# Two tiles for A's values, later output weights, a second tile turned by TensorE and a new order at the end

## The chip, the cores and the metric

The kernel runs on one core of one Trainium2 chip. The metric is the device time of one execution in microseconds, and where several runs are given, their median. TensorE (PE) multiplies, with its weight loads (PEld) running beside it; VectorE (DVE), ScalarE (ACT) and GpSimd (POOL) do the elementwise work; SyncE (SP) mostly issues transfers.

## The reference

Two attentions over the same 2048 positions, 640 wide, with 32 heads of 20, whose results are put side by side:

```python
# A: four segments of 512; causal inside a segment, plus a memory of the segments before
p = softmax(qs @ ks.T * 20**-0.5 + causal); a_dot = p @ vs
num = phi(qs) @ M;  den = phi(qs) @ z + 1e-6          # phi(t) = t + 1 if t > 0 else exp(t)
o = g * num / den + (1 - g) * a_dot                   # g = sigmoid(beta), per head
M += phi(ks).T @ vs;  z += phi(ks).sum()
A = concat(o) @ wo
# B: causal attention over a window of 256
B = softmax(where(0 <= i - j < 256, q @ k.T * 20**-0.5, -1e9)) @ v @ wo
out = concat([A, B], axis=-1)                         # 1 x 2048 x 1280, bf16
```

## The kernel before

The work is cut into eight chunks of 512 positions, A and B in turn: chunk 0 is A's first segment, chunk 7 is B's last. For each chunk PE makes q, k and v from the transposed x (`qk_job`, `v_job`), the scores of four heads at a time (`score_batch`, L814), ACT takes their exponentials from PSUM into tiles pt (L830), POOL (L869) and DVE (L847) mask them, PE multiplies them with v (`av` L883, `av_tile` L904), DVE transposes the result by 32x32 blocks (tt, L949), takes the reciprocal of the row sums (rr, L977), and POOL writes the normalised values to o (L987). A ones column beside each head's values in v yields the row sums. For A, `mem` adds the memory's part, and `dm_job` (L686) updates the memory from phi(k) and v.

A chunk's output product needs o with its features on the partitions. `final` does that through DRAM: four stores o to scr_o (L1021), one transposing transfer back (L1040, into a tile oT, which for chunk 7 is named xT), and then `final_job` multiplies with wo. In chunk 7 this is done for each of its four query tiles of 128 by itself. The last of them (qt = 3) takes another way, `last_job`: four matmuls with an identity `one` turn 128 features of o (L1121), sixteen small ones turn the other 32 (L1133), a DVE cast (L1125, into the free tile pq) and an ACT cast (L1139, into pkT) bring them to SBUF, and two halves of five matmuls each follow (`last_half`), cast by ACT (L1156) and DVE (L1159) and stored. The third tile (qt = 2) goes through DRAM and then also through `last_half`. The rows of the weights for `last_job` are in another order, so B's output weights are loaded twice: wo_B and wo_end, the latter into the place of wk_A.

A's values of a chunk lie in one tile vA, [128, 4, 696] in bf16: 16 heads in the first 348 columns, 16 in the second. `v_job` makes one half at a time: five matmuls into one of two PSUM banks, m0 and m1 (`bank`), and a DVE multiplication that empties the bank into vA (L733), four times. Then `v_squares` copies parts of that half to the tile vS by two transfers on SP (L757). A is read by `av` through `vof`, by `v_squares` and by `dm_job`. Semaphores are set by the framework from the tiles that each instruction reads and writes: instructions on the same tile wait for one another, where one of them writes.

What PE does next is written out in PLAN, a string: `k70*7` is seven steps of the job that makes the first piece of k in chunk 7, `v71` a step of the second half of its values, `o60` an output product of chunk 6 (`o72` of the third tile of chunk 7), `z0` a step of `last_job`; S or s is the next batch of scores, A the next product with v, M the next memory product. The small S and the large S differ in whether the matmuls up to the next score are done as four tiles of 32 columns (L930) or whole (L935). Jobs are generators that yield what they still wait for in the planner's model; other engines' instructions are put between PE's by the times of that model. Loads stand in a list, each with a gate (`self.known(n, what, piece)`, the modelled time of something, for wo_B the q piece 3 of chunk 2) and a due time; `next_load` issues them on SP in the order of the list.

What the change touches:

- PLAN, from the 254th us on (chunk 7's q, k and v and what comes after); before that it is as it was
- `v_job` L730, `v_squares` L750 to L757, `av` L883, `dm_job` L684 to L687, `vof` L1573 to L1576: the places that use vA and vS
- L1346 and L1347, L1357: making vA and vS, their ones columns (`v_ones`, L796 and L800) and zeros, on POOL
- L1372: wo_B's gate
- `final_job` L1054 to L1061, `last_job`, and `last` in `one_group` (L1602 to L1607): the third and the last tile

Of the kernel before, what the change touches and what calls it, by code (L numbers as in the profile page):

```python
# [10 lines left out]
BF16 = mybir.dt.bfloat16  # L11
F32 = mybir.dt.float32

P = 128
H = 32
DH = 20
# [67 lines left out]

def at_head(h):
    return VS * h + 12 * (h // 16)
# [181 lines left out]
class _K:  # L268
# [391 lines left out]
    def dm_job(self, seg, pkT, v):  # L660


        nc, f = self.nc, self.f
        yield self.known("pkT", seg)
        W = 4 * VS
        KT = self.KT
        spare = self.pkS
        nc.gpsimd.tensor_copy(
            out=spare[:].rearrange("p k (u r) -> p (k u) r", r=HD - DH),
            in_=pkT[:].rearrange("p k (u c) -> p (k u) c", c=HD)[:, :, DH:])  # L670
        there = f.on_pool(1000.0)
        own = [(lambda kt, m=m: pkT[:, kt, P * m:P * m + P], P, [m], m) for m in range(KT)]
        for some in (own, [(lambda kt, h=h: spare[:, kt, R2 * h:R2 * h + R2], R2,
                            [x for x in range(4) if MEM2[x][0] == h], None) for h in (1, 0)]):
            if some is not own:
                yield there
            yield "bank"
            dM, bi = self.bank()
            at = 0
            for lhs, rows, xs, g0 in some:  # L680

                gs = [g0] if g0 is not None else sorted(MEM2[x][1] for x in xs)
                n = W * len(gs)
                v0 = at_head(4 * gs[0])  # L684
                for kt in range(LT):
                    nc.tensor.matmul(dM[0:rows, at:at + n], lhsT=lhs(kt),  # L686
                                     rhs=v[:, kt, v0:v0 + n],  # L687
                                     start=(kt == 0), stop=(kt == LT - 1))
                f.on_pe("full", 4 * mm_ns(n), 4 * n, 0.0, 4)
                at += n  # L690
                if (rows, xs) != (some[-1][1], some[-1][2]):
                    yield 0.0

            rows = some[0][1]
            dv = dM[0:rows, 0:at].rearrange("p (x j c) -> p x j c", j=4, c=VS)
            if rows == P:
                mz = self.mz[:, 0:KT]
            else:
                mz = self.mz[0:rows, KT:].rearrange("p (b a) j c -> p a b (j c)", a=2)
                dv = dv.rearrange("p (a b) j c -> p a b (j c)", a=2)  # L700
            nc.vector.tensor_tensor(out=mz, in0=dv, in1=mz, op=ALU.add)
            self.close(bi, f.on_dve(100.0 + 1.04 * at, f.seen))
            f.open = False
        t = f.dve + 138.0
        yield self.known(2 * seg, "avs")
        blk, mz = self.blk, self.mz
        nc.gpsimd.tensor_tensor(out=blk[:, :, :, DH], in0=mz[:, :, :, DH], in1=self.bm[:],
                                op=ALU.mult)
        f.on_pool(150.0, t)
        nc.gpsimd.tensor_tensor(out=blk[:, :, :, 0:DH], in0=mz[:, :, :, 0:DH],  # L710
                                in1=self.ez[:].unsqueeze(3)
                                .to_broadcast([P, KT + 4, 4, DH]), op=ALU.mult)
        self.mark(f.on_pool(1700.0), "dm", seg)

    def v_job(self, n, half, w_ap, v, gate, needs):
        nc, f = self.nc, self.f
        for need in needs:
            yield need
        xT = self.xs[n]
        x0 = SH if gate else 0  # L720
        for tt in range(LT):
            yield "bank"
            ps, bi = self.bank()
            for kt in range(self.KT):
                self.wide(ps, xT[:, kt, x0 + tt * P:x0 + (tt + 1) * P],
                          w_ap[:, half, kt, :], 320, kt == 0, kt == self.KT - 1)
                if kt < self.KT - 1:
                    yield 0.0
            src = ps[:, 0:320].rearrange("p (h e) -> p h e", e=DH)
            dst = v[:, tt, HV * half:HV * half + 16 * VS].rearrange(  # L730
                "p (h e) -> p h e", e=VS)[:, :, 0:DH]
            if gate:
                nc.vector.tensor_tensor(  # L733
                    out=dst, in0=src,
                    in1=self.omg[:, 16 * half:16 * half + 16].unsqueeze(2)
                    .to_broadcast([P, 16, DH]), op=ALU.mult)
            else:
                nc.vector.tensor_copy(out=dst, in_=src)  # L738
            self.close(bi, f.on_dve(402.0, f.seen))
            f.open = False  # L740
        if not gate:
            self.v_ends(n, self.chunks[n][1], half, v)
        else:
            self.v_squares(n, half, v)
        self.used_x(n)

    def v_squares(self, n, half, v):


        f = self.f  # L750
        s = slice(HV * half, HV * half + HV)
        tok = v[0:SH, :, s].rearrange("p (a b) c -> p a b c", b=2)
        t = f.dve + 138.0

        def go():
            for odd in (0, 1):
                self.nc.sync.dma_start(  # L757
                    out=self.vS[SH * odd:SH * odd + SH, odd * 2:odd * 2 + 2, s],
                    in_=tok[:, :, odd, :])
                tl = f.on_dma(1, 410.0, t) + (1200.0 if n == 0 else 0.0)  # L760
            for g in range(4 * half, 4 * half + 4):
# [3 lines left out]
    def v_ends(self, n, c, half, v):  # L765
# [15 lines left out]
        def go():  # L781
# [3 lines left out]
            for g in range(4 * half, 4 * half + 4):  # L785
                self.mark(tl, n, "v", g)
        f.at(t, go)

    def v_tile(self, name, now=True):
        v = self.big.tile([P, LT, VW], BF16, name=name)  # L790
# [83 lines left out]
    def av(self, parts, g, vof):  # L874
# [4 lines left out]
        for n_, (ref, q0, nq, c0, pts) in enumerate(parts):  # L879
            v = vof(ref)  # L880
            for j in range(4):
                h = 4 * g + j
                nc.tensor.matmul(O[HD * j:HD * j + HD, q0:q0 + nq],  # L883
                                 lhsT=v[:, at_head(h):at_head(h) + HD],
                                 rhs=pts[j // 2][:, j % 2, c0:c0 + nq],
                                 start=(n_ == 0), stop=(n_ == len(parts) - 1),
                                 tile_position=(0, HD * j), skip_group_check=True)
# [160 lines left out]
    def final_job(self, n, wo, out2d, r0, col, t0, t1, there):  # L1048
# [2 lines left out]
        yield self.known("wo_A" if n % 2 == 0 else "wo_B", 0)  # L1051
        oT = self.oT[n]
        for tt in range(t0, t1):
            if n == len(self.chunks) - 1 and tt == LT - 2:  # L1054

                row = r0 + tt * P
                for hf in range(2):
                    yield "bank"
                    self.last_half(hf, lambda m: oT[:, m, tt * P:(tt + 1) * P], wo,
                                   out2d[row:row + P], col)  # L1060
                continue  # L1061
            while self.ring("ot", NOT) is None:
                self.stores[0]()
            yield self.ring("ot", NOT) - 700.0
# [40 lines left out]
        if t1 == LT:  # L1105
            self.mark(f.pe, "fin", n)

    def last_job(self, o, wo, out2d, r0, col, t):


        nc, f = self.nc, self.f
        yield t
        yield self.sc_free[-NSC]
        two = self.ps.tile([P, 2, 512], F32, name="sc", bufs=NSC)
        self.sc_free.append(f.pe + 3000.0)
        own = len(self.sc_free) - 1
        b0 = LT * (LT - 1)
        wide = two[:, 0, :].rearrange("p (j b t) -> p b j t", j=4, b=LT)
        one = self.one[:].rearrange("p (j t) -> p j t", j=4)
        for b in range(LT):  # L1120
            nc.tensor.matmul(wide[:, b], lhsT=o[:, b0 + b, 0:P], rhs=one, start=True, stop=True,  # L1121
                             skip_group_check=True)
            f.on_pe("full", mm_ns(P), P)
        oT = [self.pq[:, 0, 0:4 * P], self.pkT[:, 0, 0:P]]
        nc.vector.tensor_copy(out=oT[0], in_=two[:, 0, :])  # L1125
        self.sc_free[own] = td = f.on_dve(605.0, f.seen)
        yield self.sc_free[-NSC]
# [12 lines left out]
        self.sc_free[own] = ta = f.on_act(200.0, f.seen)  # L1140
        yield max(ta, td)
        oT = [oT[m // 4][:, P * (m % 4):][:, 0:P] for m in range(self.KT)]
        row = r0 + (LT - 1) * P
        for hf in range(2):
            yield "bank"
            self.last_half(hf, lambda m: oT[m], wo, out2d[row:row + P], col)
# [156 lines left out]
    def body(self, xA, A_wq, A_wk, A_wv, A_wo, A_beta, xB, B_wqkv, B_wo, out2d):  # L1303
# [39 lines left out]
        self.vL = big.tile([P, LT, VW], BF16, name="vL")  # L1343
        self.vU = big.tile([P, LT, VW], BF16, name="vU")
        self.vX = big.tile([P, VW], BF16, name="vX")
        self.vA = self.v_tile("vA")  # L1346
        self.vS = big.tile([P, LT, VW], BF16, name="vS")  # L1347
        self.consts_mz()
        nc.vector.memset(self.vL[:].bitcast(F32), 0.0)
        for t in (self.vU, self.vX):  # L1350
# [3 lines left out]
        nc.gpsimd.memset(self.kB[0][:, :, 0:SH], 0.0)  # L1354
        nc.gpsimd.memset(self.kB[0][:, KT:G, L:XC], 0.0)
        self.consts_ends()
        nc.gpsimd.memset(self.vS[:].bitcast(F32), 0.0)  # L1357
        f.on_pool(10500.0)
        f.on_dve(4500.0)
        k = len(self.loads)  # L1360
# [8 lines left out]
                                   None, 22000.0)  # L1369
        wo = {}  # L1370
        wo["A"] = self.load_w("wo_A", A_wo, self.known(0, "scored"), 6000.0)
        wo["B"] = self.load_w("wo_B", B_wo[0], self.known(2, "q", 3), 6000.0)  # L1372

        wo["end"] = self.load_w("wo_end", B_wo[1], self.known(NC - 1, "q", KT - 1), 9000.0,
                                self.wt["wk_A"][:].rearrange("p m k c -> p (m k c)").rearrange(
# [191 lines left out]
    def one_group(self, n, kind, c, g, what, parts, left, o_t, groups_done, scro, wo, out2d):  # L1567
# [3 lines left out]
        def vof(ref):  # L1571
            what, u = ref
            if what == "a":  # L1573
                return self.vA[:, u, :]
            if what in "st":
                return self.vS[:, 2 * (u % 2) + u // 2, :]  # L1576
            if what == "l":
                return self.vL[:, u % LT, :]
            if what == "u":
# [10 lines left out]
        if what == "tile":  # L1590
# [10 lines left out]

            def last(t):  # L1602
                if g0 == G - 4:
                    if qt == LT - 1:
                        self.fins.insert(0, self.job(self.last_job(o, wo["end"], out2d, c * L, col, t), "z0"))
                        return
                    self.final(n, o, scro[n], wo[kind], out2d, c * L, col, qt, qt + 1, t)  # L1607
            self.norm(tt, dst, False, last)
# [103 lines left out]
```

## Time and profile before

| what | us |
|---|---|
| median of three runs (332.38, 332.24, 330.19) | 332.24 |
| the profiled execution's own time | 332.54 |
| its span in the trace | 330.7 |
| busy: PE, PEld | 316.4, 176.2 |
| busy: ACT, POOL, DVE | 299.6, 265.4, 255.8 |
| granted PE clock | 1.00 of full |
| transfers: moved, packets | 47.45 MB, 76266 |

Times within the trace count from the start of the span; 1.84 us of the execution's time lie outside of it. In lists of waits a line names who waited, on what, and how long in total, how often and at most. In a timeline a line is a run of like instructions: start, duration, engine, source line, operation, tiles, count, and in brackets the idle time before it with what ended it. Engines with a q (SPq, ACTq) are queues that issue transfers. In the page the span is also cut into 40 slices of 8.27 us, with the busy share of each in tenths.

### The profile page before, as it was taken

Reading aid. Unit: us, or ns where it says so; the run is one execution under the profiler, and the core shown is the slowest. Engines: PE = TensorE matmul, PEld = TensorE weight load, DVE = VectorE, ACT = ScalarE, POOL = GpSimd, SP = SyncE. Lnnn points to the kernel's source line nnn. Section 1 sums busy time; section 2 is a strip of 40 time slices with the busy share of each in tenths; the row PEclk is TensorE's granted clock in tenths of the full one; section 3 lists DMA queues with packets and bytes.
Section 4 is the critical chain, followed back from the end, with each engine's and each line's share of the span. In section 5 each row is a group of like instructions: output and inputs, shape, how many; then the busy total and the mean of one; then the engine's idle time right before and its main releaser. Section 6 shows DMA issues by size and latency. Waiting matters only on the chain.

```text
span 330.7 us, 16968 instructions
## 1 busy us (share of the span) xinstructions
PE 316.4 (96%) x7195; PEld 176.2 (53%) x7195; DVE 255.8 (77%) x533; ACT 299.6 (91%) x333; POOL 265.4 (80%) x672
## 2 busy tenths in 40 slices
PE   7999999998999999999999999999999999999984
PEld 2454546555445455646653546456654445666652
DVE  6777767797977787999867897988777798876753
ACT  1979999998999998989999999899999999979962
POOL 8466679997759899976886999998975899989850
PEclk9999999999999999999999999999999999999999
DMA  7975945675589354165689146117868027397642
GB/s 210 388 250 135 194 138 108 150 193 159 135 214 217 67 115 132 22 141 147 138 216 174 33 86 157 50 32 154 147 181 186 14 54 185 107 233 159 109 127 80
DMA packets 76266, 47.45 MB, mean 143 GB/s; under 512 B 48382, under 2 KB 73182, under 8 KB 76190
## 3 DMA queue, kind: packets, MB, share of 16 engines
q1 hardware_dynamic: 75469, 45.71, 57.7%
q8 instruction: 56, 0.92, 1.2%
q10 hardware_dynamic: 720, 0.66, 0.7%
q14 instruction: 21, 0.16, 0.2%
HBM read 17.62 MB, written 16.96 MB: 105 GB/s over the span
## 4 chain that ended last, share of the span: by engine, by line
PE 36%; DVE 5%; ACT 3%; DMA 2%; POOL 2%; issue 1%; SPq 1%; ACTq 0%; DVEq 0%
PE m L935 19%; PE sc L814 7%; PE m L883 5%; ACT pt L830 3%; PE m L930 2%; DVE tt L949 2%; PE m L904 1%; DMA xT<-scr_o 1%; DVE pt L847 1%; DMA scr_o<-o 1%; POOL pt L869 1%; DVE kA L557 1%; POOL o L987 1%; DVE ot L1099 0%; PE m L686 0%
## 5 line engine op out<-in xcount | busy, mean ns | idle before, releaser
L830 ACT ACTIVATE pt<-sc 128x1024 bf16<-128x1024 f32 (+2 forms) x306 | 282.9, 1026 | 15.1 <-PE sc L814 12.9
L869 POOL TENSOR_SCALAR_AFFINE_SELECT pt<-pt 128x128 bf16<-128x128 bf16 (+1 forms) x512 | 178.0, 376 | 49.8 <-ACT pt L830 42.8
L949 DVE STREAM_TRANSPOSE tt<-m 128x512 f32<-128x512 f32 x88 | 61.2, 709 | 24.7 <-PE m L883 15.9
L987 POOL TENSOR_TENSOR o<-tt,rr 128x320 bf16<-128x320 f32 x64 | 48.5, 758 | 4.7 <-DVE rr L977 3.9
L814 PE MATMUL sc<-qB,kB 20*64 20x64 bf16 (+2 forms) x1728 | 39.9, 217 | 0.8 <-ACT pt L830 0.3
L935 PEld LDWEIGHTS <-xT 128*128 128x128 bf16 x296 | 26.7, 97 | 18.4 <-issue 6.1
L847 DVE TENSOR_TENSOR pt<-pt,ends 128x1024 bf16<-128x1024 bf16 (+2 forms) x50 | 36.4, 739 | 0.0
L1099 DVE CAST ot<-m 128x320 bf16<-128x320 f32 x58 | 28.1, 486 | 9.8 <-PE m L935 8.4
L814 PEld LDWEIGHTS <-kB 20*64 20x64 bf16 (+1 forms) x1728 | 22.2, 98 | 22.4 <-issue 20.5
L814 PE MATMUL sc<-qA,kA 20*64 20x64 bf16 (+4 forms) x1024 | 33.5, 237 | 0.5 <-ACT pt L830 0.4
L935 PEld LDWEIGHTS <-oT 128*128 128x128 bf16 x244 | 21.5, 97 | 12.5 <-issue 3.3
L814 PEld LDWEIGHTS <-kA 20*128 20x128 bf16 (+1 forms) x1024 | 13.4, 97 | 22.4 <-issue 21.3
L935 PE MATMUL m<-wBv,xT 128*128 128x320 bf16 x147 | 24.2, 299 | 0.9 <-DVE tt L949 0.4
L883 PE MATMUL m<-pt,vA 128*32 128x192 bf16 (+3 forms) x512 | 23.6, 274 | 0.2
L935 PE MATMUL m<-wo_A,oT 128*128 128x320 bf16 x125 | 21.0, 300 | 0.8 <-DVE kA L557 0.8
L935 PE MATMUL m<-xT,wBq 128*128 128x512 bf16 x82 | 21.4, 380 | 0.3 <-DVE tt L949 0.3
L935 PE MATMUL m<-xT,wBk 128*128 128x512 bf16 x81 | 20.7, 381 | 0.0
L935 PE MATMUL m<-wv_A,xT 128*128 128x320 bf16 x119 | 20.0, 300 | 0.2 <-DVE vA L733 0.2
L738 DVE CAST vB<-m 128x320 bf16<-128x320 f32 x32 | 15.6, 488 | 5.4 <-PE m L935 3.1
L935 PE MATMUL m<-wo_B,oT 128*128 128x320 bf16 x109 | 18.6, 300 | 0.8 <-DVE tt L949 0.4
L557 DVE CAST qB<-m 128x512 bf16<-128x512 f32 x20 | 13.8, 688 | 6.7 <-PE m L930 3.4
L935 PE MATMUL m<-xT,wk_A 128*128 128x512 bf16 x69 | 17.7, 379 | 1.2 <-DMA xT<-in_A_x_dram 1.1
(127 smaller groups left out, 460.2 us busy)
## 6 DMA issues: line engine op xcount, KB each, us to landing
out_dram<-ot SPq DMA_DIRECT2D x29, 160.0 KB
scr_o<-o SPq DMA_DIRECT2D x28, 160.0 KB
xT<-in_B_x_dram SPq DMA_DIRECT2D x8, 288.0 KB
xT<-in_A_x_dram SPq DMA_DIRECT2D x8, 256.0 KB
scr_pk<-e SPq DMA_DIRECT2D x15, 128.0 KB
vS<-vA SPq DMA_DIRECT2D x16, 87.0 KB
vL<-vB SPq DMA_DIRECT2D x8, 174.0 KB
scr_kA<-kA SPq DMA_DIRECT2D x16, 60.0 KB
```

The source lines that it names most:

```text
L557: nc.vector.tensor_copy(out=dst[:, m, at:at + L], in_=ps[:, :])
L738: nc.vector.tensor_copy(out=dst, in_=src)
L814: nc.tensor.matmul(ps[j // 2][h0:h1, j % 2, c0:c0 + nq], lhsT=k[rows, g, k0:k0 + h1 - h0], rhs=q[rows, g, q0:q0 + nq], start=True, stop=Tr ...
L830: nc.scalar.activation(out=pt[:, :, lo:hi], in_=ps[i][:, :, lo:hi], func=ACT.Exp, scale=self.scale)
L847: nc.vector.tensor_tensor(out=blk, in0=blk, in1=self.ends[:, c0, :].unsqueeze(1).unsqueeze(1) .to_broadcast([P, 2, n // SH, SH]), op=ALU.mult)
L869: nc.gpsimd.affine_select(out=blk, in_=blk, pattern=pat, compare_op=ALU.is_ge, fill=self.zero, base=base, channel_multiplier=mul)
L883: nc.tensor.matmul(O[HD * j:HD * j + HD, q0:q0 + nq], lhsT=v[:, at_head(h):at_head(h) + HD], rhs=pts[j // 2][:, j % 2, c0:c0 + nq], start= ...
L930: self.nc.tensor.matmul(ps[s, 0:n], lhsT=lhsT[:, s], rhs=rhs, start=start, stop=stop, tile_position=(0, HD * j), skip_group_check=True)
L935: self.nc.tensor.matmul(ps[:, 0:n], lhsT=lhsT, rhs=rhs, start=start, stop=stop, skip_group_check=True)
L949: self.nc.vector.transpose(out=tt[:], in_=O[:, :])
L987: nc.gpsimd.tensor_tensor(out=to[:] if add_to else to, in0=a, in1=b, op=ALU.mult)
L1099: nc.vector.tensor_copy(out=ot[:, 320 * hf:320 * hf + 320], in_=ps[:, 0:320])
```

## The change

It does four things. vA and vS become two tiles each, one for each half of 16 heads, and every use takes the half's tile with its offset. The gate of wo_B's load becomes q piece 0 of chunk 4. In chunk 7 the third tile (qt = 2) is also handed to `last_job`, with its own places in pq and pkT (second slices), the label z0 (the last tile is z1 now), and the weights wo_end; its four stores and the transposing transfer go. And the last fifth of PLAN is another order of the same kinds of steps. Before the 254th us PE's order is unchanged.

```diff
-    "A k70*2 S k70*5 v70*3 S v70*2 q70*4 s q70 A s M q70*6 s q70*4 A s k73*5 s v70*5 A s M "
...
-    "s o40*5 o50*3 s o50*2 o40*5 o50*2 s o50*3 A s o50*10 s A o50*2 s o50*9 s o50*9 s A o60*5 s "
-    "o60*5 o70*5 A o70 s o70*4 o60*5 s o60*5 o71*4 s o71*6 o60*2 s o60*6 A o60*8 A o60*4 o72*2 "
-    "z0*4 ")
+    "A k70*2 S k70*5 v70*3 S v70*2 q70*4 s q70 A M s q70*5 s A q70*5 s v70*5 k73*2 s k73*3 A s "
...
+    "A s o40*5 o50*5 s o40*5 o50*5 s A o50*4 s o50*6 s A o50*4 s o50*8 s o50*8 s A o60*5 s "
+    "o60*10 o70*5 s A o70*3 s o70*2 o60*7 s o60*8 o71*2 s o71*3 o60*2 A o60*3 z0 o71*5 o60 A "
+    "o60 z0 o60*3 z0 z1*2 z0 z1*2 ")
...
-                v0 = at_head(4 * gs[0])
+                v0 = at_head(4 * gs[0]) - HV * (gs[0] // 4)
...
-                                     rhs=v[:, kt, v0:v0 + n],
+                                     rhs=v[gs[0] // 4][:, kt, v0:v0 + n],
...
-            dst = v[:, tt, HV * half:HV * half + 16 * VS].rearrange(
+            own, c0 = (v[half], 0) if gate else (v, HV * half)
+            dst = own[:, tt, c0:c0 + 16 * VS].rearrange(
...
-        tok = v[0:SH, :, s].rearrange("p (a b) c -> p a b c", b=2)
+        tok = v[half][0:SH].rearrange("p (a b) c -> p a b c", b=2)
...
-                    out=self.vS[SH * odd:SH * odd + SH, odd * 2:odd * 2 + 2, s],
+                    out=self.vS[half][SH * odd:SH * odd + SH, odd * 2:odd * 2 + 2, :],
...
+    def half_tiles(self, name):
+        return [self.big.tile([P, LT, HV], BF16, name="%s%d" % (name, x)) for x in range(2)]
...
-            if n == len(self.chunks) - 1 and tt == LT - 2:
-                row = r0 + tt * P
-                for hf in range(2):
-                    yield "bank"
-                    self.last_half(hf, lambda m: oT[:, m, tt * P:(tt + 1) * P], wo,
-                                   out2d[row:row + P], col)
-                continue
...
-    def last_job(self, o, wo, out2d, r0, col, t):
+    def last_job(self, o, wo, out2d, r0, col, t, qt):
...
-        yield self.sc_free[-NSC]
+        yield lambda: self.sc_free[-NSC] if self.all_scored else None
...
-        b0 = LT * (LT - 1)
+        b0 = LT * qt
+        own_x = LT - 1 - qt
...
-        oT = [self.pq[:, 0, 0:4 * P], self.pkT[:, 0, 0:P]]
+        oT = [self.pq[:, own_x, 0:4 * P], self.pkT[:, own_x, 0:P]]
...
-        self.vA = self.v_tile("vA")
-        self.vS = big.tile([P, LT, VW], BF16, name="vS")
+        self.vA = self.half_tiles("vA")
+        for t in self.vA:
+            nc.gpsimd.memset(t[:, :, 0:16 * VS].rearrange("p t (h e) -> p t h e", e=VS)[
+                :, :, :, DH], 1.0)
+            nc.gpsimd.memset(t[:, :, HV - 12:HV], 1.0)
+        self.vS = self.half_tiles("vS")
...
-        wo["B"] = self.load_w("wo_B", B_wo[0], self.known(2, "q", 3), 6000.0)
+        wo["B"] = self.load_w("wo_B", B_wo[0], self.known(4, "q", 0), 6000.0)
...
-                    if qt == LT - 1:
-                        self.fins.insert(0, self.job(self.last_job(o, wo["end"], out2d, c * L, col, t), "z0"))
+                    if qt >= LT - 2:
+                        self.fins.insert(0, self.job(self.last_job(
+                            o, wo["end"], out2d, c * L, col, t, qt), "z%d" % (qt - LT + 2)))
```

More of the change, by code (lines that the diff above doesn't have):

```diff
@@ L750, in v_squares @@
         f = self.f
-        s = slice(HV * half, HV * half + HV)
-        tok = v[0:SH, :, s].rearrange("p (a b) c -> p a b c", b=2)
+        tok = v[half][0:SH].rearrange("p (a b) c -> p a b c", b=2)
         t = f.dve + 138.0
@@ L881, in av @@
             for j in range(4):
-                h = 4 * g + j
+                at = at_head(4 * g + j) - (HV * (g // 4) if ref[0] in "ast" else 0)
                 nc.tensor.matmul(O[HD * j:HD * j + HD, q0:q0 + nq],
-                                 lhsT=v[:, at_head(h):at_head(h) + HD],
+                                 lhsT=v[:, at:at + HD],
                                  rhs=pts[j // 2][:, j % 2, c0:c0 + nq],
@@ L1142, in last_job @@
         oT = [oT[m // 4][:, P * (m % 4):][:, 0:P] for m in range(self.KT)]
-        row = r0 + (LT - 1) * P
+        row = r0 + qt * P
         for hf in range(2):
@@ L1356, in body @@
         self.consts_ends()
-        nc.gpsimd.memset(self.vS[:].bitcast(F32), 0.0)
+        for t in self.vS:
+            nc.gpsimd.memset(t[:].bitcast(F32), 0.0)
         f.on_pool(10500.0)
@@ L1573, in vof @@
             if what == "a":
-                return self.vA[:, u, :]
+                return self.vA[g // 4][:, u, :]
             if what in "st":
-                return self.vS[:, 2 * (u % 2) + u // 2, :]
+                return self.vS[g // 4][:, 2 * (u % 2) + u // 2, :]
             if what == "l":
```

4 rows, old and new, of the table PLAN are left out of this document.

## The prediction

> **What bounds the kernel now.** I read the page first, then the waits over the whole span, then the waits and the timeline of 72 to 90 us and of 310 to 331 us, where the diff acts, and at last the busy time by windows.
>
> ```profile
> PE 316.4 (96%) x7195; PEld 176.2 (53%) x7195; DVE 255.8 (77%) x533; ACT 299.6 (91%) x333; POOL 265.4 (80%) x672
> PE   7999999998999999999999999999999999999984
> PEclk9999999999999999999999999999999999999999
> ```
>
> TensorE (PE) is busy for 316.4 of 330.7 us, nearly evenly, at the full granted clock. So time can come back only from the about 14 us in which PE stands, 4 of them before its first x and in the last writes, or from fewer matmuls, and the change removes no matmul. ScalarE (ACT), at 91%, is close behind: what PE gains in a stretch where ACT has no gap is lost again at the next score that needs a free bank. The waits name the stalls:
>
> ```profile
> DVE vA L733 <- DMA vS<-vA: 1.5, 1, 1.5
> PEld L883 <- DVE vA L733: 2.2, 3, 1.5
> ACT e L577 <- DVE kA L557: 0.9, 1, 0.9
> PE m L935 <- DVE kA L557: 0.8, 2, 0.5
> PE m L935 <- DMA xT<-scr_o: 0.8, 1, 0.8
> PE m L935 <- DVE pq L1125: 0.6, 1, 0.6
> ```
>
> The columns are total us, times and longest. The first line is one wait of VectorE (DVE) for a transfer; the next three are its consequences. The timeline places them (start, duration, in brackets the idle time before and its releaser):
>
> ```profile
> 73.17 2.07 SPq L319 DMA_DIRECT2D wo_B<-in_B_wo_dram  x2
> 75.33 1.33 SPq L757 DMA_DIRECT2D vS<-vA  x2
> 79.51 0.49 DVE L733 TENSOR_TENSOR vA<-m,omg 128x320 bf16<-128x320 f32 x1 [1.49 <-DMA vS<-vA]
> 80.06 0.29 PE L883 MATMUL m<-pt,vX 128*32 128x256 bf16 x4 [1.01 <-DVE vA L733]
> 81.91 0.57 PE L935 MATMUL m<-wo_A,oT 128*128 128x320 bf16 x3 [0.47 <-DVE kA L557]
> 81.95 1.06 ACT L577 ACTIVATE e<-kA 128x1024 bf16<-128x1024 bf16 x1 [0.93 <-DVE kA L557]
> 87.42 1.94 ACT L830 ACTIVATE pt<-sc 128x1024 bf16<-128x1024 f32 x2 [0.50 <-PE sc L814]
> ```
>
> SP, the transfer queue, issues B's 800 KB of output weights at 73.17 and only then the copy vS<-vA of half 0. That copy reads the tile vA, DVE's next instruction writes half 1 of the same tile, and so DVE stands until the copy has landed. PE then stands for a bank that DVE would have emptied (1.01), and again for kA (0.47), which DVE, without a gap from 79.51 to 87.72, reaches late. The other place is the end:
>
> ```profile
> 315.68 0.72 PE L935 MATMUL m<-wo_B,xT 128*128 128x320 bf16 x4 [0.84 <-DMA xT<-scr_o]
> 316.84 3.77 ACT L830 ACTIVATE pt<-sc 128x1024 bf16<-128x1024 f32 x4 [0.81 <-PE sc L814]
> 317.94 3.54 POOL L869 TENSOR_SCALAR_AFFINE_SELECT pt<-pt 128x256 bf16<-128x256 bf16 x8 [2.94 <-ACT pt L830]
> 321.40 0.12 PEld L904 LDWEIGHTS <-vB 128*32 128x32 bf16 x8 [0.26 <-DVE tt L949]
> 323.49 0.73 POOL L987 TENSOR_TENSOR o<-tt,rr 128x320 bf16<-128x320 f32 x1 [0.95 <-DVE rr L977]
> 324.26 0.23 PEld L1121 LDWEIGHTS <-o 128*128 128x128 bf16 x4 [0.32 <-POOL o L987]
> 324.72 0.68 DVE L1125 CAST pq<-sc 128x512 bf16<-128x512 f32 x1
> 325.46 0.72 PE L935 MATMUL m<-wk_A,pq 128*128 128x320 bf16 x4 [0.56 <-DVE pq L1125]
> ```
>
> PE waits for the transposed second tile (0.84), the last scores come late, so do the exponentials, POOL's masks, the last product with v, its normalisation, and the last tile's turning. Between the two places lies a stretch that ACT holds:
>
> ```profile
> 240.00:293.00 53.00, 52.13 (x1145) 28.15 (x1131) 41.91 (x91) 52.24 (x56) 45.49 (x120) 1.00 0.54 132
> ```
>
> Busy time here stands as PE, PEld, DVE, ACT, POOL: both PE and ACT are over 98% full.
>
> **Part 1, tiles for the halves.** DVE's write of half 1 no longer waits for the copy of half 0. The matmul that fills its bank is done by 77.5, so DVE goes on at 78.02, 1.49 earlier. The bank is empty at 78.51, before PE asks at 79.05: the 1.01 goes. kA, done at 81.86, comes at 80.37; PE asks at 81.44 - 1.01 = 80.43: the 0.47 goes too. That is 1.48. The bound above is DVE's own 1.49 and PE's two small stands after it (0.36 at 84.79 and 0.16 at 85.99), so 2.0; ACT can follow by its gaps, 0.93 + 0.50 = 1.43, before it is full. I take 1.4, the nearest limit. The bound below is 0, if the shift is met by a later wait of like size. The other fifteen copies cost nothing now: the list of waits has this one alone. In the prelude POOL does four memsets for vA instead of three and two for vS instead of one (0.67 + 0.51 and 1.25 in all before, same bytes); an additional one is 0.1 to 0.7, its work ends at 7.95 and its first mask starts at 10.28 after 2.34 of idleness: hidden, and 0 if that cover held only 0.7.
>
> **Part 2, wo_B later.** Two SP issues (2.07) and 800 KB leave 73.17 and go behind the last x load of the fifth chunk, 127.02 by the old times, where SP then has nothing until 138.68 and the transfer engines stand at a share of 0.30 over 120 to 140. At the old pace from issue to landing (the second half's issue ended at 75.23, the copy behind it had landed by 79.51) it is there by about 131 to 133; PE first reads it at 149.6. Cover 16 us or more: 0. At 73 the copy vS could now leave 2.1 earlier; with part 1 nobody waits for it at 79.51, so the gain is not counted twice. Either part alone should end the 1.49. SP's moves behind it (scr_qA at 76.75 and what follows) come up to 2.1 earlier: bounded by 0 and the 0.2 that PEld waits for scr_kA; taken as 0.
>
> The Trainium skill, "DMA: Bandwidth & Descriptors", Rules for kernel authors, advises to issue a transfer early and to wait on it late; by that the old place of wo_B, 76 us ahead of its use, is the better one, and part 2 could only lose. The trace disagrees here: the early place is what the copy stood behind.
>
> **Part 3, the third query tile by TensorE.** Added on PE: 4 matmuls of L1121 (0.40) and 16 of L1133 (0.30), as the last tile has now, 0.70. Added on DVE a cast of 0.68 like L1125's, on ACT one of 0.27 like L1139's. Removed on SP: four stores of scr_o (315.04 to 316.92) and a transpose issue (318.30 to 319.94). That transfer is hidden now: issued like the second tile's (issue 311.50, landed 315.63, 4.13) it lands near 322.43, and PE asks at 322.75. So nothing is saved by the removal itself. The 0.70 lies before the last tile's turning, where PE stands 0.32 for POOL's o, 0.18 and 0.26 earlier. The third tile's second half, 5 matmuls or 0.69, is kept for the 0.56 in which PE waits for DVE's cast. Cost between 0 and 0.70; the end is worked out with part 4.
>
> The Trainium skill, "Perfetto Trace Analysis", Transposes, wants such turns done as transposes, not as a standard matmul, which these 20 are. By it PE pays for arithmetic that it could skip, at most the 0.70, and the sum would be 0.7 smaller; the waits above say that most of the 0.70 falls into stands.
>
> **Part 4, the new order from 254 us on.** The numbers of matmuls and of changes between tile shapes stay as they are. To 311 us I give it 0: ACT runs from 240.23 to 292.84 without a break. The bound above is PE's short stands for ACT there, about 1.2; below, -0.7, one score asked late by as much as a batch (16 to 64 matmuls, up to 0.7). In the tail the second tile's ten matmuls move behind the last scores, so its transposed tile (315.63) is asked for at about 316.5: the 0.84 goes, and the 0.18 after it. The last scores start at 316.9 instead of 317.92, ACT's last four exponentials run without the 0.81, so ACT and POOL end about 1.15 earlier (POOL at 320.3 instead of 321.48). PE, from 317.3: 5 matmuls (0.137 each, 0.68), first product 0.86, 3 matmuls, turn 0.40, 6 matmuls, then the last product with v at 320.6 instead of 321.40. Its chain is unchanged (2.86 from that start to L1121): turning at 323.46, done 324.16, cast by 324.6; the third tile's second half ends at 324.85, and the last ten start there instead of 325.46. Gain 0.6. Bounds: 1.1 (the masks' whole shift) and 0 (the 0.7 of part 3 uncovered).
>
> **Sum.** 1.4 + 0 + 0.6 = 2.0. The profiled execution is 332.54 (span 330.7 and 1.84 around it), 0.30 over the median of 332.24 of the three runs, which lie from 330.19 to 332.38. 332.54 - 2.0 = 330.54; against the median 330.2 us.
>
> **Rivals.**
> A, absorbed: the 1.4 is given back before 254, at ACT or at a later wait of DVE, since PE arrives early at scores whose banks are taken. For it: ACT is 91% busy. Against: ACT has its own 1.43 in the same place, and a further gap of 1.26 at 210.39. Only the 0.6 is left, or less: 331.7.
> B, the order gives more: PE's stands for ACT to 311 (1.2) go too, ACT's gap of 1.95 at 294.79 shows that it would take the work. 332.24 - 3.3 = 328.9 and less.
> C, slower: the third tile's turning is put by DVE and PE ahead of the last tile's. Place: DVE's cast (0.68) between the last product and its transpose, and PE's 0.70 ahead of that product, with scores before 311 each asked late by up to 0.7. It decides if the first turning is ready only after about 320.6; each is then on the path in full, 1.4, with the 0.6 lost and the 0.84 kept since the second tile's data are late again: 332.24 - 1.4 + 1.4 + 0.8, about 333; 334.4 if part 1 is absorbed too, over 335.6 with two late scores on top. Against: that tile's o is written by 315.04, as its stores show, long before.
> D, part 1 does not do what it says: the wait at 79.51 remains through another dependency. With only the tail, 331.6; counted with A.
>
> **How the numbers follow.** Forecast (330 to 331.2) 0.5, A and D 0.22, B 0.16, C 0.12 (its worst 0.08). Within 1%, about what a measurement here can tell from no change, is 328.9 to 335.6. Forecast, A, D and most of C lie in it. Faster by over 1%: B's 0.16 and a little of the forecast, 0.2; slower by over 1%: the worst of C, 0.08; same 0.72. The range 328.3 to 332.7 leaves out the deep end of B and most of C.
>
> **What would show it.** Right if no DVE wait for vS<-vA remains, kA's wait at 81.4 is gone and PE reaches its 254th us 1.4 earlier; if wo_B is issued near 126 with no PE wait at its first use; if the 0.84 for xT is gone and the last ten matmuls follow the third tile's second half directly. Wrong if PE waits on ACT's pt before 254 grow by about 1 (A), if waits on ACT to 311 shrink by over 1 (B), or if DVE's second pq cast sits ahead of the last transpose (C).

## The result

The changed kernel takes 330.48 us in the median of 22 runs (329.76 to 331.63), against 332.42 us for the kernel before, also of 22 (329.65 to 336.27). The ratio is 0.9946, with a 95% interval of 0.9929 to 0.9963: 1.9 us less, a gain of half a per cent, clear of the noise and smaller than 1%. The forecast was 330.2. The profiled execution of the changed kernel took 330.69 with a span of 329.0, against 332.54 and 330.7. Medians are of all runs; ratios, and medians of several sets together, leave out the runs that lie more than 1.5% above the fastest of their kernel.

The total came out as forecast, its two terms did not. The early parts alone reach the whole gain, though I gave them 1.4, and of the 0.6 that I added for the end nothing shows on top of them.

### The profile page after: what moved, and what is told of

Same layout as the page of the kernel before. It is cut to its first block, busy times and chain, and to the rows that moved or that the text cites. A ratio compares the mean times of both kernels' runs of the same rounds, so it can differ in the third digit from the quotient of the medians.

```text
span 329.0 us, 16969 instructions
## 1 busy us (share of the span) xinstructions
PE 314.1 (95%) x7180; PEld 177.2 (54%) x7215; DVE 257.7 (78%) x534; ACT 299.8 (91%) x334; POOL 266.2 (81%) x674
## 3 DMA queue, kind: packets, MB, share of 16 engines
q1 hardware_dynamic: 74221, 45.38, 57.2%
## 4 chain that ended last, share of the span: by engine, by line
PE 48%; POOL 9%; ACT 7%; DVE 5%; issue 4%; POOLq 0%; ACTq 0%; DVEq 0%
PE m L939 25%; PE sc L818 10%; PE m L887 7%; ACT pt L834 6%; POOL pt L873 6%; PE m L934 5%; DVE tt L953 3%; POOL o L991 2%; PE m L908 1%; POOL u L991 1%; DVE pt L851 1%; PE m L686 0%; POOL rr L972 0%; ACT e L577 0%; POOL MZ L710 0%
## 5 line engine op out<-in xcount | busy, mean ns | idle before, releaser
L939 PEld LDWEIGHTS <-xT 128*128 128x128 bf16 x286 | 25.8, 97 | 17.7 <-issue 6.8
L939 PE MATMUL m<-xT,wBq 128*128 128x512 bf16 x73 | 20.6, 380 | 0.9 <-DVE tt L953 0.3
L939 PE MATMUL m<-xT,wBk 128*128 128x512 bf16 x70 | 19.6, 380 | 0.7 <-issue 0.3
L557 DVE CAST kB<-m 128x512 bf16<-128x512 f32 x20 | 13.6, 680 | 6.7 <-PE m L939 5.7
```

Of the source, the lines that this page charges most:

```text
L557: nc.vector.tensor_copy(out=dst[:, m, at:at + L], in_=ps[:, :])
L939: self.nc.tensor.matmul(ps[:, 0:n], lhsT=lhsT, rhs=rhs, start=start, stop=stop, skip_group_check=True)
```

## The profile after

The page first:

```profile
span 329.0 us, 16969 instructions
PE 314.1 (95%) x7180; PEld 177.2 (54%) x7215; DVE 257.7 (78%) x534; ACT 299.8 (91%) x334; POOL 266.2 (81%) x674
```

35 matmul records are missing from this trace (7180 against 7215 weight loads), so its PE time is some us too low; stages are measured on the weight loads below. The timeline around the old stall, with the same columns as before:

```profile
73.50 0.70 PE L939 MATMUL m<-wv_A,xT 128*128 128x320 bf16 x4 [0.48 <-DVE qA L557]
74.48 1.66 SPq L757 DMA_DIRECT2D vS<-vA  x2
77.97 0.48 DVE L734 TENSOR_TENSOR vA<-m,omg 128x320 bf16<-128x320 f32 x1
124.88 0.91 SPq L319 DMA_DIRECT2D wo_B<-in_B_wo_dram  x2
```

The copy vS<-vA leaves SP 0.85 earlier, nothing stands ahead of it, and DVE's next write of vA (third line) has no idle time in brackets any more; before, it stood 1.49 for the copy. The weights are issued at 124.88, and no wait for them appears anywhere. The first line is new, a wait of 0.48 for DVE's qA; it did not come again in other profiles of the same order. Busy time of 78 to 82 us (PE, PEld, DVE, ACT, POOL), the kernel before and then the changed one:

```profile
78.00:82.00 4.00, 2.52 (x122) 1.64 (x122) 2.48 (x7) 3.07 (x5) 2.68 (x7) 1.00 0.45 111
```

```profile
78.00:82.00 4.00, 3.91 (x130) 2.54 (x131) 3.97 (x12) 4.00 (x6) 3.50 (x8) 1.00 0.39 69
```

PE goes from 2.52 to 3.91 of 4.00, and DVE and ACT are full. The end of the changed kernel:

```profile
310.56 7.48 ACT L834 ACTIVATE pt<-sc 128x1024 bf16<-128x1024 f32 x8 [0.44 <-PE sc L818]
315.37 3.53 POOL L873 TENSOR_SCALAR_AFFINE_SELECT pt<-pt 128x256 bf16<-128x256 bf16 x8 [1.32 <-PE m L939]
318.34 0.69 DVE L1122 CAST pq<-sc 128x512 bf16<-128x512 f32 x1
319.04 0.12 PEld L908 LDWEIGHTS <-vB 128*32 128x32 bf16 x8 [0.26 <-DVE pq L1122]
321.90 0.40 PE L1118 MATMUL sc<-one,o 128*128 128x128 bf16 x4 [0.33 <-POOL o L991]
322.47 0.72 PE L939 MATMUL m<-wk_A,pq 128*128 128x320 bf16 x4
325.74 0.34 ACTq L1169 DMA_DIRECT2D out_dram<-ot  x1
```

ACT's two gaps (0.80 and 0.81) have become one of 0.44; the last eight exponentials run together, and POOL's last masks end at 318.90 instead of 321.48. The last product with v follows at 319.04 (321.40 before); of these 2.36 us, 1.36 are there already at the 5491st weight load (see below), ahead of the new order. The third tile's second half starts at 322.47, and PE no longer waits for the cast.

To see where time is won and lost in any of the kernels, I cut each trace at the same instructions. PE's order is equal in all of them up to 254 us, so the 16th, 1901st and 5491st weight load are the same work. The stages are a: 16th to 1901st load (the old stall lies in it); b: to the 5491st; c: to the start of the last product with v; d: to PE's last matmul; e: to the end of the issue of the last store; f: to the end of the span. All in us, each from one trace:

| kernel | 16th load at | a | b | c | d | e | f | c to f |
|---|---|---|---|---|---|---|---|---|
| before | 6.38 | 91.44 | 155.56 | 68.02 | 5.59 | 1.32 | 2.42 | 77.35 |
| changed | 5.86 | 90.11 | 156.05 | 67.03 | 5.69 | 1.34 | 2.89 | 76.95 |
| e1 halves alone | 6.22 | 89.55 | 155.41 | 67.42 | 5.59 | 1.31 | 2.43 | 76.75 |
| e2 gate alone | 5.87 | 89.55 | 156.02 | 67.32 | 5.59 | 1.32 | 2.42 | 76.65 |
| e3 halves and gate | 5.91 | 89.55 | 155.83 | 67.44 | 5.58 | 1.33 | 2.41 | 76.76 |
| e4 end alone | 5.92 | 91.13 | 156.11 | 67.06 | 5.70 | 1.33 | 2.89 | 76.98 |
| e5 new order, third tile by DMA | 5.89 | 89.67 | 155.90 | 66.80 | 8.20 | 1.25 | 2.43 | 78.68 |
| e6 old order, third tile turned | 6.08 | 89.56 | 156.49 | 66.82 | 6.77 | 1.40 | 2.86 | 77.85 |
| e7 new order from 309 us only | 6.33 | 89.61 | 155.80 | 67.01 | 5.70 | 1.33 | 2.89 | 76.93 |
| e8 changed again | 5.96 | 89.61 | 156.66 | 67.02 | 5.70 | 1.33 | 2.87 | 76.92 |
| e9 changed, more on SP | 5.86 | 89.55 | 155.90 | 67.08 | 5.70 | 1.33 | 2.43 | 76.54 |
| e10 second tile later | 5.81 | 90.01 | 155.74 | 67.12 | 5.59 | 1.32 | 2.42 | 76.45 |
| e11 halves and gate again | 6.25 | 89.84 | 156.68 | 67.28 | 5.59 | 1.32 | 2.42 | 76.61 |

Stage b is the same work in all rows and differs by 1.3 from trace to trace, and the first x comes in anywhere within 0.6: this is what a single time of these kernels can't see through. Where nothing in a stage was changed, the others repeat within about 0.1 to 0.6, but for the c of 68.02.

## Experiments on the early part

Each kernel was timed in 12 runs; the kernel before beside them had medians of 332.67 (e1 to e4), 332.20 (e5 to e8) and 332.22 (e9 to e11).

**e1, the halves alone.** Everything on vA and vS from the change, and nothing else of it:

```diff
-        self.vA = self.v_tile("vA")
-        self.vS = big.tile([P, LT, VW], BF16, name="vS")
+        self.vA = self.half_tiles("vA")
...
+        self.vS = self.half_tiles("vS")
```

> The kernel before with only vA and vS as two tiles each; wo_B, the order and the third tile as before. Theory (the two places add up, 1.4 early and 0.6 or more at the end): DVE's 1.5 us for vS<-vA and PE's 1.0 and 0.5 behind it are gone, time 1.0 to 1.5 below the kernel before. Rival (the early gain is given back before 254 us, all comes from the end): the wait is gone and the time is within 0.4 of the kernel before. Rival (this part does nothing): the wait at about 79 us is still there.

330.25 us, ratio 0.9929 (0.9907 to 0.9951), 2.4 below: more than either theory said. The wait is gone and stage a is 1.9 shorter. With stage b at 155.41 nothing is given back before 254 in this trace. Over all traces stage b is 156.04 in the mean of the eleven without the wait and 155.84 in the two with it, so the rival of a gain that is all given back falls; a part of some tenths is inside the scatter of b.

**e2, the gate alone.**

```diff
-        wo["B"] = self.load_w("wo_B", B_wo[0], self.known(2, "q", 3), 6000.0)
+        wo["B"] = self.load_w("wo_B", B_wo[0], self.known(4, "q", 0), 6000.0)
```

> The kernel before with only wo_B's gate moved to chunk 4. Theory: the two transfers vS<-vA leave SP at about 74.4 instead of 75.3 and land near 78.3 instead of 79.5, so DVE's wait shrinks from 1.5 to 0.4 or less, and the time falls by 1.0 to 1.4, nearly as with the halves alone. Rival (only the shared tile costs; where the weights are loaded is hidden): wait and time as before, within 0.4.

330.69 us, ratio 0.9979 (0.9947 to 1.0011). The time alone is unclear, since its interval takes in no change; the trace is not. The tile is still shared and DVE does not wait, and stage a is that of e1 to the hundredth:

```profile
73.89 1.72 SPq L757 DMA_DIRECT2D vS<-vA  x2
77.45 0.48 DVE L733 TENSOR_TENSOR vA<-m,omg 128x320 bf16<-128x320 f32 x1
```

From the end of the copy's issue (75.61) to DVE's start it is 1.84 at most here. In e4 (the end alone, below), where the weights stay ahead, the issue starts as early, but the copy takes 3.15 from the end of its issue (75.79) to DVE's release:

```profile
72.73 0.92 SPq L319 DMA_DIRECT2D wo_B<-in_B_wo_dram  x2
73.94 1.85 SPq L757 DMA_DIRECT2D vS<-vA  x2
78.94 0.49 DVE L733 TENSOR_TENSOR vA<-m,omg 128x320 bf16<-128x320 f32 x1 [1.35 <-DMA vS<-vA]
```

So in e4 it is not the place in SP's queue that costs (the issues start within 0.05 of each other) but the 800 KB ahead of it on the transfer engines: 1.3 us or more. The copy's own packets run from 75.18 to 76.86 in e2 and from 76.17 to 78.51 in e4. In the profile of the kernel before the queue costs too: there the two issues of the weights took 2.07 instead of 0.92, the copy's issue started at 75.33, and its packets ran from 77.50 to 79.02.

**e3, both.**

> Both early parts, with the order and the third tile as before. Theory: they take away the same wait, so 1.4 below the kernel before, like either alone, within 0.4 of the better of the two. Rival (each has a gain of its own): about twice that, 2.5 or more below.

330.06 us, ratio 0.9933 (0.9905 to 0.9961); run again as e11, it had 330.82 and 0.9950 (0.9922 to 0.9978). Stage a is 89.55 and 89.84. The two parts remove the same wait; the second adds nothing to the first.

> The early parts alone again, beside the other two on the same chip. Theory (they are the whole gain, the end gives nothing on top): 329.8 to 330.6, not above the changed kernel's 330.48 to 330.79. Rival (the earlier 330.06 was chance and the end is worth its forecast 0.6): 331.0 or more.

The 330.82 is 0.22 above the theory's 329.8 to 330.6 (0.03 above the changed kernel's 330.79), and 0.2 short of the rival's 331.0: by itself inconclusive. The 23 runs of e3 and e11 together have a median of 330.29, the 34 runs of the changed kernel (with e8) 330.56. The end adds nothing that these runs can tell; a difference of some half a us either way would be lost in their scatter.

## Experiments on the end

**e4, the end alone**: the new order and the third tile by TensorE, the rest as before.

> The new order from 254 us on and the third tile by TensorE, with vA and vS whole and wo_B early as before. Theory: DVE's 1.5 and PE's 1.0 and 0.5 at 79 to 82 us stay, and the time is 0.5 to 1.0 below the kernel before, all of it after 311 us. Rival (the end brings the whole change): 1.6 to 2.0 below.

332.07 us, ratio 0.9990 (0.9964 to 1.0016): 0.6 in the medians, not clear of no change. In the trace, stages c to f fall from 77.35 to 76.98, which is 0.4.

**e8, the changed kernel again.**

> The changed kernel itself, beside the others on the same chip. Theory (with the early parts in place the end is worth 0 to 0.6): 329.6 to 330.6, level with the early parts alone (330.06). Rival (the end is worth its forecast 0.6 or more on top): 329.4 or less.

330.79 us, ratio 0.9953 (0.9924 to 0.9983): 0.2 above the theory's range and far from the rival's 329.4. Stage a is 89.61: the 90.11 of the first profile, with its wait of 0.48 for qA, was chance. Against the early parts alone the rows show what the end does: c is 0.3 to 0.4 shorter (67.02 against 67.44 and 67.28), d is 0.1 longer, and f is 0.46 longer in every kernel with the turned third tile but e9.

**e5, the new order without the TensorE way**: the changed kernel with the third tile through DRAM.

```diff
-    "o60*10 o70*5 s A o70*3 s o70*2 o60*7 s o60*8 o71*2 s o71*3 o60*2 A o60*3 z0 o71*5 o60 A "
-    "o60 z0 o60*3 z0 z1*2 z0 z1*2 ")
+    "o60*10 o70*5 s A o70*3 s o70*2 o60*7 s o60*8 o71*2 s o71*3 o60*2 A o60*3 o71*5 o60 A "
+    "o60*4 o72 z0*2 o72 z0*2 ")
```

> The changed kernel with the new order, but the third tile through DRAM and the transposing transfer as before (its two halves at the places that the TensorE way's halves have). Theory (the order needs the TensorE way, because it asks for the third tile about 2 us earlier than the old order did): o is there at about 314, the stores land 3 us later and the transposing transfer 4 us after them, so PE waits about 1 us for xT near 321 and the time is 0.5 to 1.5 above the changed kernel. Rival (the third tile's way is free either way): within 0.4 of the changed kernel, and no wait for xT over 0.3.

333.19 us, ratio 1.0026 (0.9993 to 1.0059), 2.4 above e8, where 0.5 to 1.5 was expected; in the traces c to f is 1.8 longer. The wait is 3.2, not 1:

```profile
313.51 1.76 SPq L1025 DMA_DIRECT2D scr_o<-o  x4
318.48 1.21 SPq L1044 DMA_TRANSPOSE xT<-scr_o  x1
322.94 0.85 PE L939 MATMUL m<-wo_B,xT 128*128 128x320 bf16 x5 [3.15 <-DMA xT<-scr_o]
```

Stores to 315.27, transposing transfer issued from 318.48, data at 322.9: 9.4 us from the first store to the first matmul, where PE would have come at 319.79. The new order makes this tile's o later than the old one: POOL has written it 62.0 after the 5491st weight load, and 60.1 to 60.2 in the kernel before, e3 and e11. As it stands it could not do without the TensorE way.

**e6, the TensorE way without the new order**, with the early parts; its steps follow one another in the place of the old ones.

```diff
-    "o60*5 o70*5 A o70 s o70*4 o60*5 s o60*5 o71*4 s o71*6 o60*2 s o60*6 A o60*8 A o60*4 o72*2 "
-    "z0*4 ")
+    "o60*5 o70*5 A o70 s o70*4 o60*5 s o60*5 o71*4 s o71*6 o60*2 s o60*6 A o60*8 A o60*4 z0*4 "
+    "z1*4 ")
```

> Both early parts and the third tile by TensorE, all of its steps put between the old order's last chunk-6 product and the last tile's steps. Theory (the slower rival of the prediction, brought about on purpose): DVE's cast of the turned third tile now stands between the last tile's transpose and its reciprocal, so the last turning comes about 1 us later, and the time is 0.7 to 1.4 above the kernel with the early parts alone (330.06). Rival (PE's stands cover it): within 0.4 of that.

332.37 us, ratio 1.0006 (0.9973 to 1.0038), 2.1 above the early parts alone (330.29 over both sets), which is more than the 0.7 to 1.4 expected; by the traces it is 1.1 to 1.2 from c to f, and what makes the rest of the time is open. The mechanism is there:

```profile
319.94 0.72 DVE L953 STREAM_TRANSPOSE tt<-m 128x512 f32<-128x512 f32 x1 [0.74 <-PE m L908]
320.73 0.69 DVE L1122 CAST pq<-sc 128x512 bf16<-128x512 f32 x1
321.33 0.24 DVE L981 RECIPROCAL rr<-tt 128x16 f32<-128x16 f32 x1
324.19 0.72 PE L939 MATMUL m<-wk_A,pq 128*128 128x320 bf16 x4 [0.72 <-DVE pq L1122]
```

The cast stands between the last tile's transpose and its reciprocal. From the start of the last product with v to the fourth matmul of the last turning it takes 4.06 us, and 3.04 or 3.05 in all others but e5. These 1.02 are most of the 1.18 that stage d is longer than with the early parts alone. The 1.1 from c to f is a balance: c is 0.6 shorter, d 1.2 longer, f 0.45 longer. So this is the slower rival of the prediction.

**e7, where in the new order the gain lies**: the changed kernel with the old order up to chunk 6's first output product, at about 309 us, and the new one behind it.

> The changed kernel with the old order from 254 to about 309 us (up to chunk 6's first output product) and the new one from there. Theory (the stretch to 309 us is held by ACT, so its order is worth nothing): within 0.4 of the changed kernel. Rival (the new order of that stretch matters): 0.5 to 1.2 above the changed kernel, or as much below.

330.54 us, ratio 0.9970 (0.9935 to 1.0006), against 330.79 of e8 beside it; stage c is 67.01 against 67.02. The new order of 254 to 309 us, a good part of the diff, is worth nothing that the traces show.

**e9, the longer shutdown.** Stage f is 2.86 to 2.89 with the turned third tile and 2.41 to 2.43 without. In the former the last fetch of a block of instructions on queue q14 comes in the last half us (328.71 in the changed kernel), in the latter at 318 to 322, beside work. The change takes five transfers from SP; e9 gives SP eight others:

```diff
-                self.nc.sync.dma_start(out=t[:, half], in_=w_ap[:, half])
+                for k in range(self.KT if name == "wo_end" else 1):
+                    ks = slice(k, k + 1) if name == "wo_end" else slice(0, self.KT)
+                    self.nc.sync.dma_start(out=t[:, half, ks], in_=w_ap[:, half, ks])
```

> The changed kernel with each half of wo_end loaded by five transfers instead of one: eight more instructions on SP, where the change took five away. All profiles with the third tile by TensorE so far have 2.86 to 2.89 us from the end of the last store's issue to the end of the span, and fetch a block of instructions for a queue in it; those with that tile through DRAM have 2.42 or 2.43, and that fetch comes before, beside work. Theory (fewer instructions on SP put the last fetch into the shutdown): the fetch moves ahead again, the 2.88 falls to about 2.43, time 0.4 to 0.5 below the changed kernel (330.5 to 330.8). Rival (the shutdown is longer for another reason, such as what the last stores write): 2.88 stays.

Stage f is 2.43 again, the fetch is at 324.67, and the span is the shortest of all:

```profile
span 327.8 us, 17010 instructions
```

The instructions of the shutdown show where the 0.46 lies, the changed kernel first (count, then shortest, median and longest in ns):

```profile
L1710 SPq DRAIN  x3: 7/7/116, 328.1 to 328.5; - x3
```

```profile
L1712 SPq DRAIN  x3: 7/7/7, 327.1 to 327.4; - x3
```

In the changed kernel SP's first drain starts 2.01 after the last store's issue and takes 116 ns; in e9 it starts after 1.65 (1.66 in the kernel before) and takes 7. All that follows is as much later. So SP is the engine that stands. The fetch at 328.71 comes behind this stand: it goes along with it in every profile, but it is not shown to be what SP waited for.

The time, 330.60 with a ratio of 0.9957 (0.9934 to 0.9981), does not resolve the 0.45.

**e10, one move instead of the new end**: the early parts, the third tile through DRAM, and eight of the second tile's ten products behind the last scores.

```diff
-    "... s o60*5 o71*4 s o71*6 o60*2 s o60*6 A o60*8 A o60*4 o72*2 "
+    "... s o60*9 s o60*6 o71*2 s o71*6 A o71*2 o60*6 A o60*4 o72*2 "
```

> The early parts with the old order and the third tile through DRAM, and only one move at the end: eight of the second tile's ten output matmuls (and so the first use of its transposed data) go behind chunk 6's next products. Theory (of the new end only the later use of the second tile is worth anything): the wait of 0.3 for xT goes, the last product with v starts 0.3 to 0.5 earlier than with the early parts alone (67.0 instead of 67.4 us after the 5490th weight load), and the stretch from there to the end stays 9.3, so 0.3 to 0.5 below the early parts alone. Rival (the masks of the last scores set the end, whatever PE does): no change of that start.

Stage c is 67.12 instead of 67.44 and 67.28, 0.2 to 0.3 shorter where 0.3 to 0.5 was expected, with d to f as short as before: 76.45 from c to f, the least of all. The time is 330.71, ratio 0.9961 (0.9935 to 0.9986): again nothing that 12 runs can tell from the early parts or from the changed kernel.

## Why the prediction was right, point by point

- What bounds the kernel: PE's stands, not its work. Right; as far as the runs can tell, the whole gain comes from the stands of stage a.
- Part 1, that DVE would go on at once and that PE's 1.01 and 0.47 would go. Right. The size was too small for stage a, which falls by 1.9 against the kernel before (91.44 to 89.55) and by 1.6 between the means of the two traces with the wait (91.44 and 91.13) and of the eleven without (89.69); 1.4 was forecast and 2.0 was the bound above. Up to the 254th us, with stage b and its scatter, the means differ by 1.4. The step that was too tight is the cap: "ACT can follow by its gaps, 0.93 + 0.50 = 1.43". I missed a third gap, at 93.28 in the kernel before:

```profile
93.28 4.69 ACT L830 ACTIVATE pt<-sc 128x1024 bf16<-128x1024 f32 x5 [0.25 <-PE sc L814]
```

In e3 none of the three is left, ACT runs 12 us on end there, and PE got nearly all of its four stands (1.01 + 0.47 + 0.36 + 0.16 = 2.00):

```profile
85.36 12.08 ACT L834 ACTIVATE pt<-sc 128x1024 bf16<-128x1024 f32 x13
```

A limit by ACT there is: PE now stands 0.40 for an exponential at about 80 us, in each trace without the old wait but the first of the changed kernel. Its size is not settled: e4's trace has only the two gaps (0.80 + 0.51 = 1.31), and its stage a is 1.58 above 89.55 all the same.

- Either part alone ends the stall, and the second is not counted twice. Right (e1, e2, e3).
- Part 2, the late load costs nothing. Right: no wait for wo_B. The rule of the Trainium skill ("DMA: Bandwidth & Descriptors", Rules for kernel authors), to issue early and wait late, did not hold for this load: the early issue cost 1.3 us of a copy that somebody waited for, while its own use was 76 us off.
- Part 4, nothing before 311 us. Right (e7), to the hundredth in stage c.
- Parts 3 and 4, the end, 0.6. Wrong as a term of the sum. Inside it most steps hold: the last product comes 2.36 earlier than before, from there to the turning it is 2.86 again, and the third tile's second half fills the wait for the cast. What failed is "its chain is unchanged" taken to the end of the span, and that the xT stall of 0.84 was booked in full. Against the one profile of before the end gains 0.99 in c, and loses 0.10 in d, 0.02 in e and 0.47 in f: 0.40. And with the early parts the old end has less to give: the wait for xT is 0.29 in e3 (0.84 before), and stage c 67.3 to 67.4 instead of 68.02. So on top of the early parts the end is worth 0.4 - 0.1 - 0.46, about -0.2 in the traces and nothing in the times. The line that shows it, in e3:

```profile
313.00 0.72 PE L939 MATMUL m<-wo_B,xT 128*128 128x320 bf16 x4 [0.29 <-DMA xT<-scr_o]
```

Stage c of the old end shrinks by about as much as this wait does: by 0.58 for 0.55 in e3, by 0.74 for 0.72 in e11. The second tile's transposing transfer is issued 58.12 after the 5491st weight load in the kernel before and 57.2 to 57.7 in e1, e2, e3 and e11; in kernels with the new end it varies as much (57.27 in e4, 58.14 in e8). So the 0.84 of one trace was no fixed price; what moves the issue from trace to trace is open.

- The Trainium skill's wish for a transpose instead of a standard matmul ("Perfetto Trace Analysis", Transposes) could matter for the 0.70 of PE time; no run here shows it, since c is shorter in spite of the 0.70.
- Rivals. A and D fall by e1 and e2. B's extra gain in the order does not exist. C is real, but the changed order avoids it: its cast, at 318.34, stands ahead of the last but one reciprocal, which had time.

The two errors nearly cancel, and that is luck: 1.4 + 0.6 was forecast. By their ratios (0.9933 and 0.9950) e3 and e11 are 1.7 to 2.2 faster than the kernel before without any change at the end, and from c to f they take 76.6 to 76.8 where the kernel before took 77.35. So what I had booked for the new end is there without it, and the total fits to 0.1 although one of its terms does not exist.

## What to carry to other kernels

Two changes that remove the same wait are worth one of them, so measure each alone before the sum is written; and a gain at the end that is read off one trace of the old kernel should be read again in a trace that has the gain that comes before it. A bulk load with tens of microseconds to spare should not be issued just ahead of a small copy that an engine's next instruction depends on. When PE is fully booked, a cap by a second engine must be summed over all its gaps in the stretch, small ones too.

## What the runs showed that I had not expected

- Fewer instructions on a queue can go with a longer end. With five transfers less on SP a block of instructions is fetched in the shutdown instead of beside work, SP stands before its drain, and stage f is 0.46 longer in five profiles of five; eight other transfers on SP take it back (e9, 2.43, one profile). That SP stands is seen; that it stands for instructions is argued from this count.
- PE can stand where the profile shows nothing that it waits for. In the changed kernel's first profile it does so in the middle of a product with v ("issue" is the profile's name for such time):

```profile
160.30 0.20 PE L887 MATMUL m<-pt,vL 128*32 128x64 bf16 x1 [0.83 <-issue]
```

The same matmul waits 0.16 in the kernel before and 0.22 in e11. An 8 KB block of instructions was fetched on q14 from 159.74 to 160.21, just ahead of it, but in e8 and e11 such a fetch ends only behind the matmul's start, so the cause is not shown. Nor do these stands explain why stage b varies by 1.3 us with the same work: the three longest b (e11, e8, e6) have 0.22, 0.32 and none over 0.15.
